# Which operand stands still: the sequence DFT of a Fourier block, with the DFT matrix stationary in place of the data

## The chip, the cores and the metric

The kernel runs on one core of a Trainium2 chip. The metric is the device time of one execution in microseconds. Five engines matter here: TensorE (PE) does the matmuls, VectorE (DVE) and ScalarE (ACT) do elementwise work and move results out of the accumulators (PSUM), GpSimd (POOL) does elementwise work in SBUF alone, and SyncE (SP) issues every DMA. Each engine works through its own instructions in the order in which they were written; between engines there are semaphores.

## The reference

One layer: a Fourier mixing block and a gated feed-forward block, each behind a layer norm, on 2048 tokens of 448 columns.

```python
# x: (1, 2048, 448); layernorm(x) = (x - mean) / sqrt(var + 1e-5), over the 448 columns
xn = layernorm(x)
a = einsum("bsd,ed->bse", xn, dft_hid_re)
b = einsum("bsd,ed->bse", xn, dft_hid_im)
h = x + einsum("ts,bse->bte", dft_seq_re, a) - einsum("ts,bse->bte", dft_seq_im, b)
hn = layernorm(h)
out = h + (gelu(hn @ w_gate) * (hn @ w_up)) @ w_down        # w_gate, w_up: 448 x 1792
```

All arrays are 32-bit floats. The matrices are inputs; the kernel uses nothing of the DFT's structure.

## The kernel before

**Arithmetic.** Each 32-bit operand is split into a 16-bit high part and a 16-bit low part, the rest. ScalarE makes the high part (`hi_part`, L105), VectorE the low part (`lo_part`, L109 and L111). A product is three matmuls: high x high, high x low, low x high.

**Order of the two DFTs.** The kernel transforms along the sequence first: z = W x, with the real and the imaginary W (2048 x 2048 each), and then along the hidden axis, y = z_re C - z_im S. h = x + y.

**Sequence DFT (L346 to L442).** There are 16 chunks of 128 tokens to sum over, and before the change 4 blocks of 512 output tokens: 64 steps, step n = 16 b + c. In a step the stationary operand is a 128-column piece of `xs[c]` (x normalized, high or low), the moving one is W's 512 columns (`seq_w`). 448 columns are three pieces of 128 and one of 64. The three full pieces, real and imaginary, have an accumulator each: 18 matmuls a step (`seq_mm`, L416). The 64-column pieces of the real and the imaginary part share one accumulator, each in half of its partitions: six matmuls of 64 columns a step, done for four steps at a time (`seq_mm_rest`, L430). The result is transposed, hidden index on the partitions, which is what the hidden DFT needs as its stationary operand: `z_out` scales the accumulators and splits them into `z[b]`, 7 accumulators every 16 steps.

**Feeding it.** In each step SP loads W five steps ahead (`seq_load`, 512 KB, five buffers `wr`), ScalarE and VectorE split W three steps ahead (`seq_hi`, `seq_lo`, tiles `ws`), and in the first steps they also normalize x (`x_stats`, `x_norm`, `x_lo`). Steps 0 and 1 have their W in halves (`first_load`, `first_hi`, `first_lo`). 56 small transposes (L99) precede the first matmul.

**What else stands in the 64 steps.** Two tables say what is put where: `early[n]` before the matmuls of step n, `after[n, half]` behind each half of them. They hold
- the preparation of 14 weight tiles of the feed-forward block (`Weights`): tile k is loaded at step 13 + 3k, its sums (VectorE) are made at 17 + 3k, the splits at 18 + 3k and 19 + 3k, and the result is stored to DRAM at 19 + 3k;
- the hidden DFT of the blocks that are done: `hid_mm` (L481, 21 matmuls of 448 columns for 128 tokens), whose result is added to x in `hx` (L489), and `h_store`;
- for the first half of the tokens the layer norm, sums and splits of h (`ffn_stats`, `ffn_norm`, `ffn_sums`, `ffn_split`) and their turn by DMA transposes into `hops` (`ffn_transpose`, L285, four for each pair of 128-token groups).

A pair of 128-token groups is numbered p or (b, j), p = 2b + j, p from 0 to 7.

**After it.** The last block's four hidden products stand behind the loop (L1001), and then 56 `GateUp` tiles follow, t = 0 to 55 (gate and up projection by Strassen-like products X, Y and Z of 256 moving columns, L716). `GateUp.open` makes the first products of X and Y and two intermediate sums, `u1` (from X, ScalarE) and `u2` (VectorE); X's next product waits until u1 has read X. From t = 14 the down projection (L664) runs beside them.

**Memory.** SBUF is given out by pools. Pool `dft` (the right end of SBUF, 229,344 bytes down) belongs to the DFT; when it is closed, `fpool` takes the same end. A pool lays out its tags in the order of first use. `fpool` has `reuse_waits="tile"`: a tile in it waits for the tiles of the old pool that lie where it lies, each until its last reader is done.

Of the kernel before, what the change touches and what calls it, by code (L numbers as in the profile page):

```python
# [13 lines left out]
P = 128  # L14
# [6 lines left out]
TB = 512  # L21
NB = S // TB
# [10 lines left out]
def kernel(  # L33
# [9 lines left out]

# [54 lines left out]
    for k in range(56):  # L98
        PE.transpose(pw[:, k % 8, :], ident, ident)  # L99
# [246 lines left out]
    def x_stats(i):  # L346
        mv = stats(xt[i], f"x{i}")
        norm_x[i] = mv, root(mv, f"x{i}")

    def x_norm(i):  # L350
        mv, sd = norm_x.pop(i)
        xn = xt[i][:, 0, :]
        normed(xn, xn, mv, rstd(mv, sd, f"x{i}"), 0)
        xs[i] = dft.tile([P, 2, D], F16, name=f"xs{i}")
        hi_part(xs[i][:, 0], xn)

    def x_lo(i):
        lo_part(xs[i][:, 1], xt[i][:, 0, :], xs[i][:, 0])
# [3 lines left out]

    wr, ws = {}, {}

    def seq_load(n):
        wr[n] = dft.tile([P, 8 * P], F32, tag="wr", bufs=5, name=f"wr{n}")
        b, q, jj = n // NT, n // 2 % 8, n % 2
        nc.sync.dma_start(wr[n], w_seq[(2 * b + jj) * 8 + q])

    def seq_hi(n):  # L370
        if n % 2 == 0:
            ws[n // 2] = dft.tile([P, 2, 2, 8 * P], F16, tag="ws", bufs=4, name=f"ws{n // 2}")
        hi_part(ws[n // 2][:, 0, n % 2], wr[n], D_SC)

    def seq_lo(n):
        t = ws[n // 2][:, :, n % 2]
        lo_part(t[:, 1], wr[n], t[:, 0], D_SC)


    def first_load(c, jj):  # L380
        if c == 0:
            wr[jj] = dft.tile([P, 8 * P], F32, tag="wr", bufs=5, name=f"wr{jj}")
        if c == jj == 0:
            ws[0] = dft.tile([P, 2, 2, 8 * P], F16, tag="ws", bufs=4, name="ws0")
        cols = slice(c * P, (c + 1) * P)
        nc.sync.dma_start(wr[jj].rearrange("p (b t) -> p b t", b=4)[:, :, cols], w_seq[jj * 8][:, :, cols])

    def first_views(c, jj):
        cols = slice(c * P, (c + 1) * P)
        ts = [wr[jj], ws[0][:, 0, jj], ws[0][:, 1, jj]]  # L390
        return [t.rearrange("p (b t) -> p b t", b=4)[:, :, cols] for t in ts]
# [9 lines left out]
    def seq_w(n, l, part):  # L401

        t = ws[n // 2][:, l].rearrange("p a (r g c t) -> p r c a g t", r=2, g=2, c=2)
        return t[:, part, n % 2]

    TERMS = ((0, 0), (1, 0), (0, 1))
    acc = {}

    def seq_mm(n, parts, terms=range(3)):

        b, c = divmod(n, NT)
        for part in parts:
            for k in range(3):
                for m in terms:
                    lx, lw = TERMS[m]
                    PE.matmul(  # L416
                        acc[b, 3 * part + k],
                        xs[c][:, lx, k * P : (k + 1) * P],
# [760 lines left out]
```

## Time and profile before

| | |
|---|---|
| median of 3 runs | 723.78 us (723.65 to 723.87) |
| profiled execution, its own time | 724.0 us |
| its span, first to last instruction | 722.2 us |
| PE busy | 716.9 us (99%) |
| PE weight loads (beside the matmuls) | 497.6 us (69%) |
| VectorE busy | 520.5 us (72%) |
| ScalarE busy | 276.8 us (38%) |
| GpSimd busy | 237.4 us (33%) |
| DMA queue of the program | 138.99 MB, 58.0% of 16 engines |
| granted TensorE clock, mean | 1.000 |

How to read the profile's lines. A group's line names the source line, engine and operation, what is written and read (out<-in), partitions x elements and type, and the count; then busy time in us, mean ns of one, the idle time of that engine just before, and what ended it ("<-"). A line of the timeline has start and length in us, and "x2" where equal neighbours were merged. In the chain that ended last each piece is followed back to what released it. "SPq" is SP's queue of DMA issues; "to landing" is the time from a DMA's issue to its end. L105, L109 and L111 are helpers and appear for many tiles, so the tile's name tells them apart.

### The profile page before, as it was taken

How to read it: one execution, taken by the hardware profiler on the slowest of the kernel's cores; microseconds unless marked ns; L12 is line 12 of the kernel's file. 1: busy time of each engine (PE TensorE's matmuls, PEld its weight loads, DVE VectorE, ACT ScalarE, POOL GpSimd, SP SyncE). 2: the span in 40 equal slices, each digit the busy share in tenths (PEclk: the TensorE clock that was granted, in tenths of full speed). 3: DMA queues.
4: the chain of work that ended last, by engine and by line, in shares of the span. 5: the costliest groups of instructions: out<-in, count | busy, mean ns of one | idle time of the engine just before them, and what ended most of it. 6: DMA issues, size and time to landing. Idle time of an engine off the chain costs nothing.

```text
span 722.2 us, 13457 instructions
## 1 busy us (share of the span) xinstructions
PE 716.9 (99%) x5309; PEld 497.6 (69%) x5309; DVE 520.5 (72%) x1074; ACT 276.8 (38%) x542; POOL 237.4 (33%) x277
## 2 busy tenths in 40 slices
PE   9999999999999999999999999999999999999998
PEld 5444444444444444444488889999999999999998
DVE  6888657486674956440567768788787877988787
ACT  4444704157132452130344443443444324444331
POOL 0000000000000001000137855577676776858541
PEclk9999999999999999999999999999999999999999
DMA  8766565678657876712643454756538486565401
GB/s 278 229 226 218 185 216 194 201 218 275 233 197 213 292 234 248 291 58 71 253 151 132 158 207 174 199 180 201 187 120 250 164 215 229 172 238 205 154 26 52
DMA packets 63663, 139.84 MB, mean 194 GB/s; under 512 B 30320, under 2 KB 39664, under 8 KB 63600
## 3 DMA queue, kind: packets, MB, share of 16 engines
q1 hardware_dynamic: 63600, 138.99, 58.0%
q8 instruction: 41, 0.67, 0.4%
q14 instruction: 22, 0.18, 0.1%
HBM read 112.23 MB, written 20.19 MB: 183 GB/s over the span
## 4 chain that ended last, share of the span: by engine, by line
PE 96%; DMA 2%; DVE 1%; ACT 0%; issue 0%; SPq 0%; DVEq 0%
PE acc L416 33%; PE pY L716 14%; PE acc_d L664 11%; PE pZ L716 9%; PE pX L716 9%; PE y L481 9%; PE acc L430 6%; PE last_a L921 2%; PE last_X L879 1%; PE last_tr L879 1%; DMA x<-in_x_dram 1%; DMA wr<-in_w_seq_dram 0%; DVE ws L111 0%; PE last_Y L921 0%; DVE xs L109 0%
## 5 line engine op out<-in xcount | busy, mean ns | idle before, releaser
L416 PE MATMUL acc<-ws,xs 128*128 128x512 f16 x1152 | 254.2, 379 | 0.6 <-DVE xs L109 0.3
L416 PEld LDWEIGHTS <-xs 128*128 128x128 f16 x1152 | 111.2, 98 | 139.4 <-issue 6.1
L716 PEld LDWEIGHTS <-gw 128*128 128x128 f16 x1911 | 186.6, 98 | 19.6 <-issue 0.7
L203 POOL TENSOR_TENSOR wd_s<-wd 128x448 f32<-128x448 f32 x7 | 7.9, 1134 | 351.9 <-DVE gu_w L111 274.1
L716 PE MATMUL pY<-hops,gw 128*128 128x256 f16 x833 | 114.0, 273 | 0.3 <-DVE u L726 0.2
L664 PE MATMUL acc_d<-wd,dn_w 128*128 128x224 f16 x882 | 105.1, 259 | 0.0
L111 DVE SCALAR_TENSOR_TENSOR ws<-wr,ws 128x1024 f16<-128x1024 f32 (+1 forms) x66 | 77.9, 1187 | 15.3 <-ACT ws L105 15.3
L105 ACT ACTIVATE ws<-wr 128x1024 f16<-128x1024 f32 (+1 forms) x66 | 66.2, 1020 | 58.1 <-DMA wr<-in_w_seq_dram 28.7
L664 PEld LDWEIGHTS <-dn_w 128*128 128x128 f16 x882 | 85.1, 98 | 2.8
L716 PE MATMUL pX<-hops,gw 128*128 128x256 f16 x539 | 74.9, 273 | 0.0
L716 PE MATMUL pZ<-hops,gw 128*128 128x256 f16 x539 | 73.7, 273 | 0.0
L726 DVE SCALAR_TENSOR_TENSOR u<-pY,u 128x256 f32<-128x256 f32 x112 | 46.9, 419 | 28.6 <-ACT c L790 18.6
L481 PE MATMUL y<-wh,z 128*128 128x448 f16 x336 | 65.7, 352 | 0.0
L489 DVE SCALAR_TENSOR_TENSOR hx<-y,hx 128x448 f32<-128x448 f32 x16 | 10.0, 624 | 76.2 <-PE y L481 76.2
L754 ACT ACTIVATE u<-pX 128x256 f32<-128x256 f32 x56 | 21.4, 383 | 89.1 <-PE pX L716 89.0
L481 PEld LDWEIGHTS <-z 128*128 128x128 f16 x336 | 32.8, 98 | 31.6 <-issue 0.4
L109 DVE TENSOR_TENSOR dn_w<-dn_s,dn_w 128x640 f16<-128x640 f32 x42 | 53.0, 1261 | 1.4 <-ACT dn_w L105 1.0
L783 POOL TENSOR_TENSOR hh<-hh,g 128x256 f32<-128x256 f32 x42 | 31.0, 739 | 64.3 <-DVE hh L726 50.7
L767 ACT ACTIVATE g<-pX 128x256 f32<-128x256 f32 x56 | 21.5, 384 | 75.0 <-PE pX L716 69.7
L792 POOL TENSOR_TENSOR hh<-hh,c 128x256 f32<-128x256 f32 x42 | 40.5, 964 | 17.1 <-ACT c L790 17.1
L430 PE MATMUL acc<-ws,xs 128*64 128x512 f16 x384 | 44.7, 381 | 0.0
L810 POOL TENSOR_TENSOR dn_s<-hh 128x256 f32<-128x256 f32 x42 | 43.4, 1034 | 0.0
(115 smaller groups left out, 862.8 us busy)
## 6 DMA issues: line engine op xcount, KB each, us to landing
gw<-w_dram SPq DMA_DIRECT2D x49, 896.0 KB, 4.8
wr<-in_w_seq_dram SPq DMA_DIRECT2D x62, 512.0 KB, 5.9
w_dram<-gu_w SPq DMA_DIRECT2D x14, 896.0 KB, 4.7
gu_raw<-in_w_gu_dram SPq DMA_DIRECT2D x28, 384.0 KB, 5.6
wd<-in_w_down_dram SPq DMA_DIRECT2D x14, 448.0 KB, 5.1
x<-in_x_dram SPq DMA_DIRECT2D x16, 224.0 KB, 2.7
hx<-in_x_dram SPq DMA_DIRECT2D x8, 448.0 KB, 6.9
h_dram<-hx SPq DMA_DIRECT2D x8, 448.0 KB, 3.1
```

The source lines that it names most:

```text
L105: A.activation(dst, src, AF.Copy, scale=scale)
L109: V.tensor_sub(dst, src, hi)
L111: V.scalar_tensor_tensor(dst, src, scale, hi, op0=ALU.mult, op1=ALU.subtract)
L416: PE.matmul(acc[b, 3 * part + k], xs[c][:, lx, k * P : (k + 1) * P], seq_w(n, lw, part), start=c == 0 and m == 0, stop=c == NT - 1 and m == 2,
L430: PE.matmul(acc[b, 6][64 * part : 64 * part + 64, :], xs[c][:, lx, 3 * P :], seq_w(n, lw, part), start=c == 0 and m == 0, stop=c == NT - 1 ...
L481: PE.matmul(y[:, :D], z[b][:, lz, k, i * P : (i + 1) * P], wh[:, lw, k, :], start=k == 0 and m == 0, stop=k == 6 and m == 2,)
L664: PE.matmul(acc[k // 2][:, k % 2 * HD : (k % 2 + 1) * HD], a_of(la, a), b_of(lb, b), start=first and m == 0 and k % 2 == 0, stop=last and ...
L716: PE.matmul(ps, w[:, wl, wa + ws, :], ops[:, m + ms, :], start=first and n == 0, stop=last and n == len(terms) - 1, skip_group_check=True,)
L726: V.scalar_tensor_tensor(dst, ps, SC, other, op0=ALU.mult, op1=ALU.add)
L783: G.tensor_mul(c21, c21, self.g1)
L792: G.tensor_mul(c22, c22, self.c12)
L810: G.tensor_sub(s[:, 2:4], t[:, 1:4:2], t[:, 0:4:2])
```

## The change

The operands of the sequence DFT change places. A tile of W (128 x 128) is now stationary, and all 448 columns of x move, high or low: 24 matmuls a step, 448 columns each, none of half width. The result has tokens on its partitions.

- Pairs 0 and 1 are summed together in steps 0 to 15 (eight accumulators, the eighth in the bank of the hidden DFT), two chunks of x for every two tiles of W. After that each pair has eight steps: four for the real part, four for the imaginary part, two accumulators each. W's tiles are loaded in two DMAs of 2 KB rows.
- `z_out` writes rows into `zs` (every four steps, two accumulators), and `z_turn` turns a pair's rows into `z` by four DMA transposes on SP's queue. The pair's hidden products follow two steps later.
- x's high part comes from x by one activation with scale and bias, x itself is normalized by another (for chunk 0 by VectorE), the terms come in another order, and 48 small transposes are left of 56.
- wh is ordered like the new z (real part, then imaginary part), in three pieces.
- Of the hidden products behind the loop those of pair 6 move into it, and pair 7's go between GateUp tiles 2 and 3. `down_prep` starts one tile later. `u2`, `g1`, `u3`, `c12` and the drain's copies move from pool `late` to `fpool`, and `late` opens at t = 3.

```diff
-    for k in range(56):
+    for k in range(48):
         PE.transpose(pw[:, k % 8, :], ident, ident)
...
+    def x_hi(i):
+        r = norm_x[i][2]
+        xs[i] = dft.tile([P, 2, D], F16, name=f"xs{i}")
+        A.activation(xs[i][:, 0], xt[i][:, 0, :], AF.Identity, scale=r[:, 3:4], bias=r[:, 4:5])
...
+    N_STEPS = NT + 8 * (NP - 2)
     def seq_load(n):
         wr[n] = dft.tile([P, 8 * P], F32, tag="wr", bufs=5, name=f"wr{n}")
-        b, q, jj = n // NT, n // 2 % 8, n % 2
-        nc.sync.dma_start(wr[n], w_seq[(2 * b + jj) * 8 + q])
+        if n < NT:
+            nc.sync.dma_start(wr[n].rearrange("p (b t) -> p b t", b=4), w_seq[8 * (n % 2) + n // 2])
+            return
+        p, part, qq = step_of(n)
+        for i in range(2):
+            dst = wr[n][:, i * 4 * P : (i + 1) * 4 * P].rearrange("p (g t) -> p g t", g=2)
+            nc.sync.dma_start(dst, w_seq[8 * p + 2 * qq + i][:, 2 * part : 2 * part + 2, :])
+    def ws_tile(n):
+        ws[n] = dft.tile([P, 2, 8 * P], F16, tag="ws", bufs=6, name=f"ws{n}")
...
-    def seq_mm(n, parts, terms=range(3)):
...
-    def seq_mm_rest(ns):
...
+    def seq_mm(key, w, block, c, terms=range(3)):
+        for m in terms:
+            lw, lx = TERMS[m]
+            PE.matmul(
+                acc[key][:, :D],
+                w[:, lw, block * P : (block + 1) * P],
+                xs[c][:, lx, :],
+                start=c == 0 and m == 0,
+                stop=c == NT - 1 and m == 2,
+            )
+    def z_out(p, part, g):
+        if p not in zs:
+            zs[p] = dft.tile([P, 2, 2, 2 * D], F16, tag="zs", bufs=2, name=f"zs{p}")
         sc = 1.0 / (X_SC * D_SC)
+        ps = acc.pop((p, part, g))[:, :D]
+        hi, lo = [zs[p][:, g, l, part * D : (part + 1) * D] for l in range(2)]
+        hi_part(hi, ps, sc)
+        lo_part(lo, ps, hi, sc)
+    def z_turn(p):
+        z[p] = hidp.tile([P, 2, 7, 2 * P], F16, tag="z", name=f"z{p}")
+        for g in range(2):
+            for l in range(2):
+                nc.sync.dma_start_transpose(z[p][:, l, :, g * P : (g + 1) * P], zs[p][:, g, l, :])
...
-    for b in range(NB):
-        for j in range(2):
-            n = (b + 1) * NT + 1 + 6 * j
...
-            for g in range(2):
-                at(after, (n + 2 * g, 0), lambda b=b, i=2 * j + g: hid_mm(b, i, ps_tr, "tr"))
...
+    for p in range(NP - 1):
+        b, j = divmod(p, 2)
+        n = (16, 21)[p] if p < 2 else 8 * p + 8
+        at(early, n - 1, lambda b=b, j=j: h_tile(b, j))
+        at(after, (n, 0), lambda p=p: z_turn(p))
+        for g in range(2):
+            at(after, (n + 2 + g, 0), lambda p=p, g=g: hid_mm(p, g))
+        at(early, n + 4, lambda b=b, j=j: ffn_stats(b, j, hp[b, j]))
+        at(early, n + 4, lambda b=b, j=j: h_store(b, j))
+        if b < 2:
+            at(early, n + 4, lambda b=b, j=j: ffn_norm(b, j, hp[b, j]))
+            at(early, n + 5, lambda b=b, j=j: ffn_sums(b, j))
+            at(early, n + 6, lambda b=b, j=j: ffn_split(b, j))
+            for k in range(4):
+                at(after, (n + 7 + k // 2, k % 2), lambda b=b, j=j, k=k: ffn_transpose(b, j, (k,)))
...
+        for half in range(2):
+            for key, unit, block, c, terms in one[half * len(one) // 2 : (half + 1) * len(one) // 2]:
+                seq_mm(key, ws[unit], block, c, terms)
+                if c == NT - 1 and 2 in terms and (n < NT or block in (5, 7)):
+                    z_out(*key)
+            for what in after.get((n, half), ()):
                 what()
+    z_turn(NP - 1)
...
     def ftile(tag, bufs, name, n=TQ):
-        return (fpool if tag == "u1" else late).tile([P, n], F32, tag=tag, bufs=bufs, name=name)
+        return fpool.tile([P, n], F32, tag=tag, bufs=bufs, name=name)
...
-    for i in range(4):
-        if i < 2:
-            down_prep(i)
-        hid_mm(NB - 1, i, *((ps_tr, "tr"), (ps_seq, "mm"))[i % 2])
...
+    down_prep(0)
...
+            if t in (2, 3):
+                hid_mm(NP - 1, t - 2)
+                ffn_moments(NB - 1, 1, hp[NB - 1, 1], t - 2)
+            if t == 3:
+                h_store(NB - 1, 1)
+                ffn_rstd(NB - 1, 1)
+                hid.close()
+                late = ctx.enter_context(tc.tile_pool(name="late", bufs=1, reuse_waits="tile"))
```

More of the change, by code (lines that the diff above doesn't have):

```diff
@@ L399, in first_lo @@
         lo_part(lo, src, hi, D_SC)
[L401 to L406, printed above, removed]
+    TERMS = ((0, 0), (0, 1), (1, 0))
     acc = {}
[L409 to L422 removed]
```

213 lines of the change are left out of this document (105 added, 108 removed).

## The prediction

> **What bounds the kernel now.** I read the page first: busy time, clock row, chain that ended last.
>
> ```profile
> span 722.2 us, 13457 instructions
> PE 716.9 (99%) x5309; PEld 497.6 (69%) x5309; DVE 520.5 (72%) x1074; ACT 276.8 (38%) x542; POOL 237.4 (33%) x277
> PEclk9999999999999999999999999999999999999999
> PE 96%; DMA 2%; DVE 1%; ACT 0%; issue 0%; SPq 0%; DVEq 0%
> ```
>
> TensorE is busy 716.9 of 722.2 us at the full granted clock, and 96% of the chain is PE. So the time falls by what PE no longer executes, and rises by every stretch in which PE is made to wait. The profiled execution took 724.0 us (its span and 1.8 us around it), against a median of 723.78 for the runs shown. The sum is made on 724.0. Within 0.2% (1.45 us) I count as no change, which is about what a measurement of this kernel can tell.
>
> Next the groups of instructions. The "mean ns of one" is a latency of overlapping matmuls, so I divide the busy time by the count, and check that in the chain, where a run of equal matmuls stands with its length.
>
> ```profile
> L416 PE MATMUL acc<-ws,xs 128*128 128x512 f16 x1152 | 254.2, 379 | 0.6 <-DVE xs L109 0.3 <-ACT xs L105 0.2
> L481 PE MATMUL y<-wh,z 128*128 128x448 f16 x336 | 65.7, 352 | 0.0
> L430 PE MATMUL acc<-ws,xs 128*64 128x512 f16 x384 | 44.7, 381 | 0.0
> ```
> ```profile
> 44.70 15.65 PE acc L416 x72
> 60.35 2.71 PE acc L430 x24
> 135.98 3.97 PE y L481 x21
> ```
>
> The chain gives 15.65/72 = 217.4 ns for a 512-column matmul, 2.71/12 = 226 ns for a pair of half-column ones (a pair takes little more than one full product), and 3.97/21 = 189.0 ns for a 448-column one. The last form has a 128x128 stationary operand changed for every matmul and 448 contiguous moving columns, among the same transfers: it is just the form that the new sequence DFT takes.
>
> **The change part by part: the DFT's matmuls.** Before, four steps are 72 matmuls and 12 pairs: 15.65 + 2.71 = 18.36 us, 4.59 a step, 293.8 us for 64. After, a step is 8 blocks x 3 terms = 24 matmuls of 448 columns, 24 x 0.189 = 4.54 us, 290.3 for 64. In columns it is a draw (1152 x 512 + 192 x 512 = 1536 x 448). All that is won is the price of a column: 217.4/512 = 0.425 ns (in the pairs 0.441) against 189.0/448 = 0.422. That is **-3.5 us**. Bounds: 0, if the dearer column belongs to the stage's traffic and stays, and -7, if moving x is as much cheaper again; I take the 448-column row itself.
>
> A sentence by itself: the Trainium skill, "TensorE: Matmul & The Clock Gate" (section "Wait — 56ns, not 53.3ns?"), gives N/2.4 + 2.5 ns for a warm matmul of N columns, thus 215.8 and 189.2 ns. By it the stage would go from 1344 x 215.8 = 290.0 to 1536 x 189.2 = 290.6 us, no gain at all; the 448-column row agrees with it, the 512-column row does not.
>
> **The start.**
>
> ```profile
> 6.68 8.09 PE L416 MATMUL acc<-ws,xs 128*128 128x512 f16 x36 [0.21 <-ACT xs L105]
> 16.12 4.50 PE L416 MATMUL acc<-ws,xs 128*128 128x512 f16 x19
> 20.89 3.84 PE L416 MATMUL acc<-ws,xs 128*128 128x512 f16 x17 [0.27 <-DVE xs L109]
> 26.08 15.91 PE L416 MATMUL acc<-ws,xs 128*128 128x512 f16 x72
> ```
> ```profile
> 4.69 0.63 ACT L105 ACTIVATE ws<-wr 128x512 f16<-128x512 f32 x1
> 5.19 0.16 DVE L137 SCALAR_TENSOR_TENSOR r_x<-r_x 128x1 f32<-128x1 f32 x1
> 6.06 0.56 ACT L105 ACTIVATE xs<-x 128x448 f16<-128x448 f32 x1
> L224 ACT ACTIVATE xn_h<-hx,nb_h,r_h 128x448 f32<-128x448 f32 x8 | 5.7, 754 | 2.3 <-DVE nb_h L222 2.2
> ```
>
> Steps 0 to 3 last from 6.68 to 26.08, 19.40 us against 18.36 at the steady rate: 1.04 us of waits for x. The new order wants one W half and x's high part for the first matmul, and takes that part from x itself by an Identity activation (with scale and bias, 754 ns in its only row) instead of a normalization on VectorE and a 0.56 us copy. r_x ends at 5.35, W's first half at 5.32, so it runs 5.4 to 6.15: PE starts 0.5 us sooner. VectorE sheds the normalization of every later x as well, and ScalarE, 38% busy by the page, has room for it. I expect one wait of 0.3 us to stay (step 1, W's second columns). **-1.2 us** (0 to -1.8). The eight warming transposes less only end before x is ready.
>
> **The turn of z.** Before, z leaves PSUM in the layout that the hidden DFT needs, and its products stand 1 to 9 steps later. Now a pair's two token blocks leave as rows (zs), four DMA transposes of 128x896 turn them, and the first hidden product is due 2.5 steps, 11.3 us, after the pair's last matmul. z's evictions keep their volume (28 x 512 against 32 x 448 columns), at the rows
>
> ```profile
> L105 ACT ACTIVATE z<-acc 128x512 f16<-128x512 f32 x28 | 16.7, 597 | 34.6 <-PE acc L416 25.1 <-PE acc L430 8.5
> L111 DVE SCALAR_TENSOR_TENSOR z<-acc,z 128x512 f16<-128x512 f32 x28 | 18.2, 690 | 28.2 <-ACT z L105 28.2
> ```
>
> but they now come every four steps, not every sixteen, and each holds VectorE in its order until PE ends that step. What lies between two of them must fit four steps, 18.15 us. I take pair 3, whose turn stands after step 31 beside the FFN work of pair 2. VectorE has in steps 28 to 31 what these rows span (from one W low part to the third after it: three W low parts, one Weights tile's sums and two splits, one pair's statistics, norm, sums and low parts; 118.04 - 103.64 = 14.40 us), and another W low part (1.21) and pair of Weights splits (1.28):
>
> ```profile
> 103.64 1.21 DVE L111 SCALAR_TENSOR_TENSOR ws<-wr,ws 128x1024 f16<-128x1024 f32 x1
> 114.75 1.28 DVE L111 SCALAR_TENSOR_TENSOR gu_w<-gu_s,gu_w 128x512 f16<-128x512 f32 x2
> 118.04 1.21 DVE L111 SCALAR_TENSOR_TENSOR ws<-wr,ws 128x1024 f16<-128x1024 f32 x1
> ```
>
> 16.9 us, from about 1.2 us after step 27 (the eviction above), with some 0.5 us of waits for ScalarE's high parts (an estimate): done 0.5 us after step 31's end. Only then can SP go on: its queue has, ahead of z's transposes, the store of that Weights tile, the next tile's two loads, hx, two of pair 2's transposes, W's two loads and a third transpose. Their pitch, from the queue's own rows:
>
> ```profile
> 98.24 0.76 SPq L474 DMA_DIRECT2D hx<-in_x_dram  x1
> 104.12 1.10 SPq L368 DMA_DIRECT2D wr<-in_w_seq_dram  x2
> 116.06 0.33 SPq L337 DMA_DIRECT2D w_dram<-gu_w  x1
> 116.43 1.38 SPq L304 DMA_DIRECT2D gu_raw<-in_w_gu_dram  x2
> 117.86 0.78 SPq L368 DMA_DIRECT2D wr<-in_w_seq_dram  x1
> 141.01 2.62 SPq L285 DMA_TRANSPOSE hops<-xs  x2
> ```
>
> 0.4 + 1.4 + 0.5 + 2 x 1.35 + 1.1 + 1.35 = 7.4; then z's high half 1.35; its low half is issued at 0.5 + 7.4 + 1.35 = 9.3 us after step 31. From issue to landing:
>
> ```profile
> L285 SPq DMA_TRANSPOSE hops<-xs x32: 1216/1442/4272, 118.7 to 590.6; - x32
> DMA to landing us min/median/max: 2.4/6.0/8.4
> ```
>
> With the median 6.0 it lands at 15.3, due 11.3: **+4.0 us** of an idle PE (0.4 at 2.4, 6.4 at 8.4; transposes whose issue stretches to 4.27 make it more). Pair 4, after step 39, has no transposes of pair 3 ahead but one, yet the store in SP's way belongs to step 40: VectorE ends it about 1.3 (evictions) + 1.2 (W) + 0.4 (wait for ScalarE) + 1.3 (splits) = 4.2 us after step 39; 4.2 + 0.4 + 1.4 + 1.35 + 1.35 = 8.7, + 6.0 = 14.7: **+3.4 us** (0 to 5.8). Pairs 0, 1, 5 and 6 have no FFN split or store beside their turn; pair 2 has one transpose ahead and lands 1 to 2 us in time. W's loads sit behind the blocked queue too, but are issued five steps ahead: no cost, as long as a burst takes under 20 us. None of these can be a gain: before, PE doesn't wait there. That W now comes in 2 KB rows by twice as many issues costs SP 0.5 us a step and PE nothing.
>
> **The end of the DFT.** Before, the four last hidden products (16 us) lie between DFT and GateUp:
>
> ```profile
> 348.11 2.10 SPq L607 DMA_DIRECT2D gw_first<-w_dram  x4
> 349.31 16.06 PE L481 MATMUL y<-wh,z 128*128 128x448 f16 x84
> L754 ACT ACTIVATE u<-pX 128x256 f32<-128x256 f32 x56 | 21.4, 383 | 89.1 <-PE pX L716 89.0
> 369.19 1.20 PE pY L716 x11
> ```
>
> Now GateUp(0) follows at once, two products move to t = 2 and 3 unchanged, and g1, u2, u3 and c12 move to fpool. The pools hand out addresses in the order of first use. By the tiles' sizes dft ends with zs (two of 7,168 bytes) and s (5,120) below 229,344: the odd zs lies at 217,056 to 224,224. fpool's u1 begins 10,752 bytes below its end, at 218,592. So u1 and u2 of GateUp(0) are laid over zs of pair 7, whose four transposes have just begun, and must wait for all four. (That a tile here waits for the tiles beneath it and no more shows in gw_first, issued at 348.11, ahead of the DFT's end.) Call that end E. The evictions of zs take 0.05 + 0.54 + 0.6: the last low half is there at E + 1.25; SP issues at E - 1.6, - 0.3, + 1.05, + 2.4. DMA is quiet there, so I take a landing from the nearest quiet row (768 columns):
>
> ```profile
> L285 SPq DMA_TRANSPOSE hops<-xs x1: 1302/1302/1302, 141.0 to 141.0; - x1
> DMA to landing us min/median/max: 3.3/3.3/3.3
> ```
>
> 3.3, and 0.3 for one block more: E + 6.0, and u1 in 0.38: E + 6.4. PE can do 18 matmuls of 256 columns first (1.20/11 = 0.109 each, 1.96 us), then X's second product waits for u1 to have read X. **+4.4 us** (3.2 to 6.8 with the 2.4 and 6.0 landings). ScalarE's wd halves, now ahead of u1 without the hidden products' cover, lie within that wait; without it they would cost under 1 us. gw_first's loads come behind the transposes and are due 11 us later, plus the wait: hidden. The later wd steps, each one tile further back, are due only at t = 14, wh's new load order only at step 18: nothing.
>
> **The sum.** 724.0 - 3.5 - 1.2 + 4.0 + 3.4 + 4.4 = **731.1 us**, said as 731.0, +1.0%.
>
> **The rivals.** (1) *The turns are in time*: pairs 3 and 4 cost nothing because SP reaches their transposes 4 us sooner (VectorE ahead of PE at steps 31 and 39, or landings of 2 us). It decides at 11.3 us from the pair's last matmul to the landing. Then 724.0 - 4.7 + 4.4 = 723.7: no change. For it: the quiet landing of 3.3; against it: 16.9 of 18.15 us booked on VectorE in those steps. (2) *Nor is u1 held*: zs and u1 don't meet, or the transposes end within 2 us of E: 724.0 - 4.7 = 719.3, faster. With the turns late but u1 free: 726.6. (3) *The clock falls in the gaps*: three waits of 3 to 4.5 us on an engine that had none over 0.3. The start shows a slow phase:
>
> ```profile
> 1.37:2.37 1.00, 1.00 (x10) 1.00 0.55 154
> 5.37:6.37 1.00, 1.00 (x20) 1.00 0.96 250
> ```
>
> 10 to 12 transposes a us at first, 20 at the end, over 4 us: some 1.6 us lost for each time PE starts cold, up to 4.8 in all: 735.8. This trace has no gap after which one could see it. The same page of the Trainium skill (section "HAM oscillation — how this bites in real kernels") has the clock halve after an idle window of some 3.4 us; no run here shows it yet. (4) *The 512-column matmuls are no slower by shape*: no gain of 3.5 us, 734.5.
>
> **How the numbers follow.** Forecast, both turns late and the end too, 727 to 736: 0.50. Clock or columns on top of it, (3) and (4), 734 to 739: 0.14. Turns in time (1), 723.7: 0.13. Late turns but a free u1, 726.6: 0.07. Neither (2), about 719.3: 0.16. Slower are the first two and the fourth, 0.71; the same is (1), 0.13; faster is (2), 0.16. The range from 719 to 738 leaves out about half of (2) and half of (3) and (4), 0.15; the forecast's own is 727 to 736.
>
> **What would show it.** Right: y's product of pairs 3 and 4 waiting 3 to 5 us for a DMA into z, PE idle 4 us shortly after the DFT with u1 waiting for a transpose, 24 DFT matmuls in 4.54 us, PE's first DFT matmul at 6.1 to 6.3. Wrong: z's transposes landing within 11 us at each pair, no gap at GateUp(0), a clock row under 9, PE waiting for ws (then SP or DMA, not z, is the bound), or a first DFT matmul later than 6.7.

## The result: 2.3% slower, not 1%

The changed kernel takes 741.05 us (median of 5 runs, 739.49 to 741.21) against 723.78 us: 1.023 times as long, with an interval of 1.0215 to 1.0245. The prediction was 731.0 us with a range to 738. The direction was right; the size was 10 us short. The page of the changed kernel, by its span, busy time, clock row and chain:

```profile
span 739.3 us, 13609 instructions
PE 718.7 (97%) x5301; PEld 517.6 (70%) x5301; DVE 517.1 (70%) x1064; ACT 293.4 (40%) x564; POOL 236.5 (32%) x277
...
PEclk9999999999799999999999999999999999999999
...
PE 88%; SPq 4%; DMA 3%; DVE 3%; ACT 1%; issue 1%; DVEq 0%; ACTq 0%
```

TensorE is busy 718.7 us, 1.8 us more than before although its products got cheaper, and its share of the chain fell from 96 to 88%; SP's queue (SPq), DMA and VectorE take 10% of it. One slice of the clock row reads 7, where before every one read 9. So two things are to be found: waits, and matmuls that ran slowly. TensorE's timeline has both; a row is start, length, instructions and count, and in brackets the idle time before it with what ended it:

```profile
6.46 53.80 PE L443 MATMUL acc<-xs,ws 128*128 128x448 f16 x281
...
103.42 18.32 PE L443 MATMUL acc<-xs,ws 128*128 128x448 f16 x96
121.58 4.13 PE L508 MATMUL y<-wh,z 128*128 128x448 f16 x21
...
155.63 31.94 PE L443 MATMUL acc<-xs,ws 128*128 128x448 f16 x168
195.39 0.93 PE L508 MATMUL y<-wh,z 128*128 128x448 f16 x2 [7.81 <-DMA z<-zs]
196.61 6.11 PE L508 MATMUL y<-wh,z 128*128 128x448 f16 x19 [0.29 <-DMA z<-zs]
202.56 4.70 PE L443 MATMUL acc<-xs,ws 128*128 128x448 f16 x24
...
211.07 31.94 PE L443 MATMUL acc<-xs,ws 128*128 128x448 f16 x168
244.42 0.55 PE L508 MATMUL y<-wh,z 128*128 128x448 f16 x2 [1.40 <-DMA z<-zs]
...
248.82 4.70 PE L443 MATMUL acc<-xs,ws 128*128 128x448 f16 x24
...
372.36 1.23 PE L771 MATMUL pX<-hops,gu_w 128*128 128x256 f16 x5 [3.94 <-ACT u L809]
...
378.12 0.71 PE L771 MATMUL pX<-hops,gu_w 128*128 128x256 f16 x5
...
394.09 0.71 PE L771 MATMUL pY<-hops,gw_first 128*128 128x256 f16 x5 [0.81 <-DVE u L781]
...
403.92 0.71 PE L771 MATMUL pY<-hops,gw_first 128*128 128x256 f16 x5 [1.44 <-DVE u L781]
```

Read row by row, against what each should have been:

- **Rate.** From 103.42 to 121.58 96 products take 18.16 us, 189.2 ns each; 1,536 of them 290.6 us against 293.8 before: -3.2 us.
- **Start.** The first product of the DFT starts at 6.46, against 6.68: -0.2 us. From there to 90.94 the first 444 products take 84.48 us, 0.5 more than at 189.2 ns each, where before the first four steps lost 1.04: another -0.5. Together -0.7 us.
- **Pair 3.** y was due at 155.63 + 168 x 0.1892 = 187.41. It waits 7.81 us for z, runs two products, waits 0.29, and then needs 5.95 us (196.61 to 202.56) for 19 products that take 3.60 at full clock. It ends at 202.56 instead of 191.38: +11.2 us, 2.9 of them (0.55 + 2.35) slow matmuls.
- **Pair 4.** Due at 211.07 + 31.79 = 242.86, the next DFT product starts at 248.82 instead of 246.83: +2.0 us.
- **End of the DFT.** GateUp(0) starts at 366.30; after 18 products (1.97 us) X's second product was due at 368.27 and starts at 372.36. The 39 products from there to 378.12 take 5.76 us instead of 4.25. Together +5.6 us, 4.1 of wait and 1.5 of slow matmuls.
- **Units 2 and 3 of gate and up.** 0.81 and 1.44 us of waits for u: +2.3 us.

-3.2 - 0.7 + 11.2 + 2.0 + 5.6 + 2.3 = +17.2 us, against 17.1 between the spans (739.3 and 722.2).

The slow matmuls go with the granted clock. A row gives the stretch, its length, TensorE's busy time (instructions), the granted clock, then DMA's busy share and GB/s:

```profile
191.20:201.40 10.20, 5.72 (x15) 0.50 0.92 200
372.10:375.40 3.30, 3.04 (x15) 0.50 0.96 369
```

From 187.2 to 191.1, from 201.5 to 211, and on either side of the second stretch the same view gives 1.00.

**Why pair 3 was so late** is read from the chain in time order (start, length, piece) between 160 and 197 us, and from the waits of SP and ScalarE from 158 to 225 (us in total, times, longest):

```profile
164.68 2.00 SPq L284
...
172.41 2.69 DMA hops<-xs
...
181.01 0.33 SPq L336
...
191.64 1.26 SPq L466
...
193.00 3.56 DMA z<-zs
```

```profile
SPq L336 <- DVE gu_w L110: 16.8, 2, 11.6
```

```profile
ACT xs L104 <- DMA hops<-xs: 8.6, 1, 8.6
```

The store of a Weights tile (line 336) and of a pair (519) stand in SP's queue until VectorE has made their data (11.6 us ahead of the Weights store at 162.08, 5.2 ahead of the next one at 181.01), and pair 1's FFN transposes (284) stand behind the first of them, issued from 164.68 on. The last lands at 175.1. Until then ScalarE holds pair 2's split, because its tile xs is the one buffer that pair 1's transposes read: 8.6 us. VectorE waits 3.6 and 0.7 us for ScalarE, the next store waits for VectorE and leaves SP only at 181.01, 4.9 us after step 31 has ended (176.06); and z's transposes come behind that, at 191.64. Theory C calls this the ring: store, transposes, split, store. It is what the trace suggests; the runs below test it against theory A, that the FFN transposes of pairs 1 and 2, now three steps apart instead of six, crowd the queue by their number, and theory B, that the turn is slow of itself.

### The profile page after: what moved, and what is told of

It reads as the page before. It is cut to its first block, busy times and chain, and to the rows that moved or that the text cites. A ratio compares the mean times of both kernels' runs of the same rounds, so it can differ in the third digit from the quotient of the medians.

```text
span 739.3 us, 13609 instructions
## 1 busy us (share of the span) xinstructions
PE 718.7 (97%) x5301; PEld 517.6 (70%) x5301; DVE 517.1 (70%) x1064; ACT 293.4 (40%) x564; POOL 236.5 (32%) x277
## 4 chain that ended last, share of the span: by engine, by line
PE 88%; SPq 4%; DMA 3%; DVE 3%; ACT 1%; issue 1%; DVEq 0%; ACTq 0%
PE acc L443 32%; PE pY L771 14%; PE acc_d L719 11%; PE y L508 9%; PE pX L771 9%; PE pZ L771 9%; SPq L284 2%; PE last_a L976 2%; DMA x<-in_x_dram 1%; DMA z<-zs 1%; PE last_X L934 1%; PE last_tr L934 1%; SPq L303 1%; DVE ws L110 1%; DVE gu_w L110 0%
## 5 line engine op out<-in xcount | busy, mean ns | idle before, releaser
L443 PE MATMUL acc<-xs,ws 128*128 128x448 f16 x1536 | 293.4, 353 | 0.1
L443 PEld LDWEIGHTS <-ws 128*128 128x128 f16 x1536 | 150.4, 98 | 140.5 <-issue 0.6
L508 PE MATMUL y<-wh,z 128*128 128x448 f16 x336 | 69.3, 362 | 9.8 <-DMA z<-zs 9.8
L104 ACT ACTIVATE zs<-acc 128x448 f16<-128x448 f32 x32 | 17.2, 541 | 102.2 <-PE acc L443 92.8
L110 DVE SCALAR_TENSOR_TENSOR zs<-acc,zs 128x448 f16<-128x448 f32 x32 | 19.4, 623 | 48.1 <-ACT zs L104 48.0
```

Of the source, the lines that this page charges most:

```text
L104: A.activation(dst, src, AF.Copy, scale=scale)
L110: V.scalar_tensor_tensor(dst, src, scale, hi, op0=ALU.mult, op1=ALU.subtract)
L443: PE.matmul(acc[key][:, :D], w[:, lw, block * P : (block + 1) * P], xs[c][:, lx, :], start=c == 0 and m == 0, stop=c == NT - 1 and m == 2,)
L508: PE.matmul(y[:, :D], z[p][:, lz, k, g * P : (g + 1) * P], wh[:, lw, k, :], start=k == 0 and m == 0, stop=k == 6 and m == 2,)
```

## The experiments

Each kernel was timed against the kernel before on the same chip (723.78 us beside the changed kernel, 723.94 to 724.21 beside the others). "Left" is TensorE's longest waits in the profiled execution, those of the first 25 us left out.

| kernel | median us | ratio to before (interval) | left |
|---|---|---|---|
| changed kernel | 741.05 | 1.023 (1.0215 to 1.0245) | 7.81, 3.94, 1.44, 1.40 |
| hidden products later | 735.76 | 1.0163 (1.0148 to 1.0178) | 5.62, 3.93, 1.44 |
| zs elsewhere | 735.64 | 1.0165 (1.0150 to 1.0180) | 7.71, 1.45, 1.22 |
| pair 2's FFN chain later | 734.85 | 1.0143 (1.0117 to 1.0169) | 4.15, 2.11, 1.90 |
| pair 7's statistics later | 741.02 | 1.0234 (1.0217 to 1.0251) | 7.78, 3.92, 1.96 |
| stores on GpSimd | 733.55 | 1.0132 (1.0113 to 1.0150) | 3.87, 2.31, 1.45 |
| W's loads on GpSimd | 759.60 | 1.0488 (1.0473 to 1.0502) | 18.43, 6.70, 3.93 |
| combination | 723.93 | 0.9993 (0.9984 to 1.0002) | 2.04 |
| combination, statistics spread | 720.14 | 0.9947 (0.9935 to 0.9960) | under 0.3 |
| the same, FFN chain not moved | 721.16 | 0.9961 (0.9949 to 0.9973) | 3.66 |
| the same, stores on SP | 722.40 | 0.9975 (0.9963 to 0.9986) | 2.05 |
| before, W contiguous | 728.57 | 1.0062 (1.0046 to 1.0077) | 0.46 |
| before, full for half columns | 720.43 | 0.9952 (0.9938 to 0.9965) | under 0.3 |

**Hidden products later.** The turns stay; the products that need them move.

```diff
         at(after, (n, 0), lambda p=p: z_turn(p))
+        n += {3: 2, 4: 1}.get(p, 0)
         for g in range(2):
             at(after, (n + 2 + g, 0), lambda p=p, g=g: hid_mm(p, g))
```

> Pair 3's hidden products and all that follows them (moments, norm, split, its FFN transposes) stand two steps later (9.1 us of DFT), pair 4's one step later (4.5 us); the turns of z stay where they are. Theory: the 7.81 us and 1.40 us that TensorE waited for z are pure lateness, and the 2.5 us of slow matmuls after the first wait go with it, so both waits vanish, nothing else becomes late, and the time falls by 11.3 + 2.0 to about 728 us (726 to 730). Rival: the wait only moves, because what comes after the hidden products is what sets the next turn; then a wait of several us stands before another pair's products and the time stays above 735 us.

The time fell by 5.3 us to 735.76, less than half of what the theory wanted: the rival was right on the size, and both waits for z had gone all the same. What took their place, a wait of 5.62 us before the second y product, is read from VectorE's rows, ScalarE's and SP's queue:

```profile
203.92 1.23 DVE L110 SCALAR_TENSOR_TENSOR ws<-wr,ws 128x1024 f16<-128x1024 f32 x1 [7.12 <-ACT ws L104]
...
209.93 0.62 DVE L516 SCALAR_TENSOR_TENSOR hx<-y,hx 128x448 f32<-128x448 f32 x1
```

```profile
202.83 1.06 ACT L104 ACTIVATE ws<-wr 128x1024 f16<-128x1024 f32 x1 [7.45 <-DMA wr<-in_w_seq_dram]
```

```profile
198.18 1.99 SPq L399 DMA_DIRECT2D wr<-in_w_seq_dram  x4
```

The second y product reuses the first one's accumulator and waits for VectorE to add it into hx. VectorE reaches hx at 209.93 because it stood 7.12 us for ScalarE's W part, which stood 7.45 us for a load of W issued at 198.18, behind z's four transposes and one of pair 2's. In the changed kernel VectorE was just as late (it stood 7.54 us for ScalarE's W part until 194.52), hidden behind TensorE's own wait for z: time given to one consumer showed the next.

**zs elsewhere.** `zs` is allocated ahead of W's tiles, so its two buffers no longer lie under u1.

```diff
             wr[jj] = dft.tile([P, 8 * P], F32, tag="wr", bufs=5, name=f"wr{jj}")
+            if jj == 0:
+                zs_tile(0)
             ws_tile(jj)
```

> The two buffers of zs are allocated at the head of the DFT's pool, so they lie under W_down's last tiles instead of under u1; no instruction is added or taken away. Theory: u1 then waits for no transpose of zs7, the 3.94 us before X's second product fall below 1 us (ScalarE still does two down-weight parts ahead of u1), the slow matmuls behind the gap go too, and the time falls by about 5 us to 736 us (735 to 737). Rival: the next thing is just as late (another tile under u1, ScalarE's queue), the idle time stays over 2.5 us and the time over 738.5 us.

735.64 us, 5.4 less. The wait before X's second product is 0.43 us, and the five products behind it take the usual 0.55 us from start to start instead of 1.02:

```profile
367.74 0.71 PE L776 MATMUL pX<-hops,gu_w 128*128 128x256 f16 x5 [0.43 <-ACT u L814]
```

The edit adds and takes away no instruction, only addresses differ. In the changed kernel u1 itself had waited for the transposes of zs:

```profile
371.93 0.38 ACT L809 ACTIVATE u<-pX 128x256 f32<-128x256 f32 x1 [3.40 <-DMA z<-zs]
```

That u1 was held by the transposes of zs beneath it is shown by the two together.

**Pair 2's FFN chain later.**

```diff
         if b < 2:
+            n += 3 if p == 2 else 0
             at(early, n + 4, lambda b=b, j=j: ffn_norm(b, j, hp[b, j]))
```

> Pair 2's norm, sums, split and FFN transposes stand three steps later (behind the turn of z of pair 3, and six steps behind those of pair 1, as far apart as those of before); its hidden products and everything of z stay. Theory A: pair 3's z is late because the FFN transposes of pairs 1 and 2 and the waits for their one buffer stand ahead of it in the one DMA queue; then the 7.81 us fall below 1.5 us, the slow matmuls behind them go, and the time falls by 9 to 11 us to about 731 us (729.5 to 733). Theory B: the turn is late of itself (four issues of 1.3 us each and a landing of 4 us against two steps); then the 7.81 us stay within 2 us and the time stays above 738 us. Between: both shares are read from the idle time that is left.

734.85 us, 6.2 less; A had expected 731. Pair 3's wait fell from 7.81 to 2.11 us, not below 1.5; what moving the chain took away is 5.7 us of it:

```profile
189.63 0.55 PE L508 MATMUL y<-wh,z 128*128 128x448 f16 x2 [2.11 <-DMA z<-zs]
190.40 5.45 PE L508 MATMUL y<-wh,z 128*128 128x448 f16 x19 [0.21 <-DMA z<-zs]
195.68 4.70 PE L443 MATMUL acc<-xs,ws 128*128 128x448 f16 x24
```

```profile
182.17 8.37 SPq L466 DMA_TRANSPOSE z<-zs  x4
```

SP now issues z's four transposes from 182.17, not from 191.64. The four issues alone take 8.37 us, and the products behind a gap of only 2.11 us still run slowly: 19 in 5.28 us instead of 3.60. Behind pair 4's waits of 1.90 and 0.26 they don't (238.84 to 242.45, 3.61 us).

**Pair 7's statistics later.** Moments and root behind unit 8.

```diff
-                ffn_moments(NB - 1, 1, hp[NB - 1, 1], t - 2)
+            if t == 8:
+                ffn_stats(NB - 1, 1, hp[NB - 1, 1])
             if t == 3:
                 h_store(NB - 1, 1)
-                ffn_rstd(NB - 1, 1)
```

> The moments and the root of pair 7 stand behind unit 8 of gate and up instead of units 2 and 3. Theory: the 0.81 and 1.44 us that TensorE waited for u in units 2 and 3 come from the 0.8 us of moments ahead of it on VectorE and the two table loads of 1.28 us on ScalarE; they fall to under 0.5 us in all, the loads now lie beside other work, and the time falls by about 2 us to 739 us (738 to 740). Rival: the hidden product's own sum and W_down's split hold u; the idle time stays over 1.5 us in all, and the time within 1 us of 741.

741.02 us: nothing. The two waits went, and one of 1.96 us came at the new place. The theory's sum was wrong: in one lump the work had its price at this place too. Whether that is VectorE's order or ScalarE's table loads this run does not tell; the spread combination below does.

**Stores on GpSimd.** Both stores, and nothing else, are issued by another engine.

```diff
-            nc.sync.dma_start(w_dram[self.f], self.w)
+            G.dma_start(w_dram[self.f], self.w)
...
-        nc.sync.dma_start(h_dram[2 * q + j], hp[q, j])
+        G.dma_start(h_dram[2 * q + j], hp[q, j])
```

> The stores of the split gate and up weights (line 336) and of the hidden pairs (line 519) are issued by GpSimd instead of SP; nothing else changes. In the trace SP stood 7 us and more before such a store until VectorE had made gu_w, with W's loads and the transposes queued behind it, while ScalarE and VectorE waited for those loads. Theory C: this ring (store waits for VectorE, W's loads wait for the store, VectorE waits for W's loads) is what makes pair 3 late; then the 7.81 us fall below 3 us, and the time falls by 6 to 10 us to 731 to 735 us. Theory A (crowded FFN transposes and their one buffer alone): the store costs little, the 7.81 us stay above 6 us and the time above 738.5 us.

733.55 us, 7.5 less, with the FFN chains as close as ever. Pair 3's wait is gone altogether, and ScalarE no longer waits for xs's buffer at all; pair 4 waits 2.31 us, and its 21 products take 5.71 us (233.99 to 239.70) instead of 3.97:

```profile
PE y L508 <- DMA z<-zs: 2.3, 1, 2.3
```

```profile
153.22 3.91 SPq L284 DMA_TRANSPOSE hops<-xs  x2
158.32 3.05 SPq L284 DMA_TRANSPOSE hops<-xs  x2
...
181.86 5.94 SPq L466 DMA_TRANSPOSE z<-zs  x4
```

Pair 1's transposes are issued from 153.22 instead of 164.68, the last two at 158.32 instead of 171.15, and z's at 181.86 instead of 191.64. That is C's ring cut at the store. C and A aren't two causes, though: moving the chain cuts the same ring at the buffer (ScalarE doesn't wait for it in that run either), and each cut alone took 5.7 us or more from that wait. At pair 3 the number of the transposes did no harm once no waiting store stood in front of them. At pair 4 it is open: the issue of z's four took 10.38 us there (from 223.79), and what stretched it was not tried. Nor was either kind of store moved by itself. The Trainium skill, "DMA: Bandwidth & Descriptors" (section "SWDGE vs HWDGE vs iDMA"), gives plain transfers to SP or ScalarE and leaves GpSimd those that accumulate or cast; here the plain stores were better on GpSimd, by these 7.5 us, because a waiting store holds up only the queue that it is in.

**W's loads on GpSimd** instead of the stores.

```diff
-            nc.sync.dma_start(dst, w_seq[8 * p + 2 * qq + i][:, 2 * part : 2 * part + 2, :])
+            G.dma_start(dst, w_seq[8 * p + 2 * qq + i][:, 2 * part : 2 * part + 2, :])
```

> W's loads of steps 16 to 63 are issued by GpSimd instead of SP, so they stand behind neither the stores nor the transposes. Theory C: with the loads out of the ring ScalarE and VectorE no longer wait 8 to 11 us for wr around pair 3, the store comes in time, and the 7.81 us fall below 3 us: 731 to 735 us. Theory A: pair 3's turn is still queued behind the FFN transposes, which wait for the split and its buffer; the 7.81 us stay above 5 us, 737 to 741 us. A third way: GpSimd's own issue of 96 loads is slower than SP's, W comes late, TensorE waits in the DFT's own products, and the time rises above 742 us.

759.6 us, 18.6 more: a miss for all three (the third had the time above 742 us, but TensorE never waited in the DFT's own products). Taking the loads out of SP's queue did not cut the ring; the wait for the xs buffer grew:

```profile
ACT xs L104 <- DMA hops<-xs: 13.0, 1, 13.0
```

The split stood 13.0 us for its buffer (8.6 in the changed kernel), and the store behind it left SP at 184.70 instead of 181.01, 3.7 us later. Then three of pair 2's transposes took 13.54 us to issue (188.29 to 201.83), where in the changed kernel they and two loads took 7.25, and z's came at 201.93 instead of 191.64. The FFN transposes' landing went from a median of 4.7 to 7.8 us in that stretch, with W's loads now issued beside them; that these are the reason was not tried. GpSimd's own pace in issuing the loads did not show: TensorE never waited for W.

**The combination.** Hidden products of pairs 3 and 4 one step later, pair 2's chain three, zs elsewhere, stores on GpSimd, pair 7's statistics behind unit 9; where an edit differs from those above:

```diff
-        n += {3: 2, 4: 1}.get(p, 0)
+        n += {3: 1, 4: 1}.get(p, 0)
...
-            if t == 8:
+            if t == 9:
                 ffn_stats(NB - 1, 1, hp[NB - 1, 1])
```

> Together: the hidden products of pairs 3 and 4 and what follows them one step later, pair 2's FFN chain three steps later, zs at the head of the pool, the two kinds of stores on GpSimd, and the moments and root of pair 7 behind unit 9. Theory: the waits are separate and each of these takes its own away; from 741.05 go 11.3 (pair 3), 2.0 (pair 4), 5.0 (u1) and 1 to 2.3 (units 2 and 3), which gives 721 us (719 to 723.5), below the 723.8 of before by the 3.3 us that the shorter matmuls gain less the late start. Rival: VectorE's and ScalarE's streams, which ran at their limit around pair 3, put another wait in place of these (as they did with the hidden products two steps later); then a wait of over 3 us is left and the time stays above 725 us.

723.93 us, 17.1 less than the changed kernel but no better than before. The waits were separate, as the theory said, and one is left, of 2.04 us:

```profile
411.45 0.87 PE L778 MATMUL pY<-hops,gw 128*128 128x256 f16 x5 [2.04 <-DVE u L788]
```

```profile
410.98 0.41 DVE L788 SCALAR_TENSOR_TENSOR u<-pY,u 128x256 f32<-128x256 f32 x1
```

VectorE's rows: the moments from 406.08, the root's arithmetic to 408.67, then c, a W_down part of 1.32 us and a sum of 0.81 us, and only at 410.98 the u that TensorE wants. That sum falls in unit 10, so unit 9 was no good place; but behind unit 8, without the sum, the lump had cost 1.96 us too. ScalarE's two table loads of 1.28 us end at 406.30 and 409.27, well before.

**Combination, statistics spread.** One moment each ahead of the W_down parts in units 3 and 5, where VectorE had gaps of 0.95 us, the root alone behind unit 7, and the first W_down parts behind unit 0's u1.

```diff
+        if t in (3, 5):
+            ffn_moments(NB - 1, 1, hp[NB - 1, 1], (t - 3) // 2)
         if t + 1 <= 2 * NC:
             down_prep(t + 1)
...
+            if t == 7:
+                ffn_rstd(NB - 1, 1)
...
-    down_prep(0)
...
     cur.open()
+    down_prep(0)
```

> As the combination before (hidden products of pairs 3 and 4 one step later, pair 2's FFN chain three steps later, zs at the head of the pool, stores on GpSimd), but pair 7's two moments stand in the gaps of VectorE ahead of W_down's parts in units 3 and 5, its root alone behind unit 7, and the first down-weight parts behind unit 0's u1. Theory: the 2.04 us at unit 9 came from VectorE's order (1.6 us of moments, 0.7 of root, a W_down part and a sum all ahead of u), not from the table loads; spread out, no wait over 0.5 us is left, and the time falls from 723.9 to 721 us (720 to 722), a ratio to before of about 0.996. Rival: the two table loads of 1.28 us on ScalarE hold u wherever they stand; then a wait of 1.4 to 2 us stays at unit 7 or 8 and the time stays at 723 to 724 us.

720.14 us, 3.8 below before, interval 0.9935 to 0.9960. This version beats both kernels. TensorE's waits, all but one of 1.4 us before any data is there:

```profile
PE acc L450 <- DVE xs L108: 0.2, 1, 0.2
PE pY L778 <- DVE u L788: 0.2, 1, 0.2
```

The table loads are still there and cost nothing, so it was VectorE's order. With no wait left the time should be 723.9 less 3.2 and 0.7, 720.0: the account closes. (The 3.8 us against the combination are its wait of 2.04 us and 1.7 us lost behind it, where the granted clock read 0.50.)

**The same without moving the FFN chain, and with the stores on SP.** Each takes one part of the last one back.

```diff
-            n += 3 if p == 2 else 0
```

> The same without moving pair 2's FFN chain: its transposes stand again three steps behind those of pair 1. Theory C: once the stores no longer hold SP, the crowding of the FFN transposes costs little; TensorE waits for z less than 1 us in all and the time is within 1 us of the version with the chain moved. Theory A: the crowding is a cause of its own; a wait of over 2 us before the hidden products of pair 3 or 4 comes back and the time is 3 us and more longer.

```diff
-            G.dma_start(w_dram[self.f], self.w)
+            nc.sync.dma_start(w_dram[self.f], self.w)
...
-        G.dma_start(h_dram[2 * q + j], hp[q, j])
+        nc.sync.dma_start(h_dram[2 * q + j], hp[q, j])
```

> The fastest combination with both kinds of stores back on SP. Theory C (the stores' waits in SP's queue are the root of pair 3's lateness): with the FFN chain moved alone 2.11 and 1.90 us were left at pairs 3 and 4, which the one step (4.5 us) covers for z itself, but SP still waits for VectorE, W's loads behind it come late, and a wait of 2 us or more for hx or z comes back: 723 to 727 us. Theory A (crowded FFN transposes): with the chain moved and the step given no wait over 1 us is left, and the time is 720 to 721.5 us.

721.16 and 722.40 us. Without the move most runs stayed near 720 to 722.8, but the profiled one, the longest of seven at 725.48, had a wait of 3.66 us at pair 3; with the stores on SP one of 2.05 us stood at pair 4 in the profiled run (723.53 us):

```profile
203.76 5.63 PE L513 MATMUL y<-wh,z 128*128 128x448 f16 x21 [3.66 <-DVE hx L521]
```

```profile
246.36 5.82 PE L513 MATMUL y<-wh,z 128*128 128x448 f16 x21 [2.05 <-DVE hx L521]
```

Both are for hx, as with the hidden products later: just before, VectorE had stood 8.71 and 13.71 us for ScalarE's W part. So neither C nor A alone decides it: the stores are worth 2.3 us here (the intervals don't touch), the chain's place 1.0 on the median, which is not clear of noise (0.9949 to 0.9973 against 0.9935 to 0.9960), and 5 in the longest run.

**Where the 3.2 us of the products come from.** Two runs of the kernel before. In the first W's moving columns are read as one run of 512:

```diff
-        t = ws[n // 2][:, l].rearrange("p a (r g c t) -> p r c a g t", r=2, g=2, c=2)
-        return t[:, part, n % 2]
+        return ws[n // 2][:, l, n % 2, part * 512 : part * 512 + 512]
```

> The kernel before with W's moving columns read as one run of 512 instead of four runs of 128 (so it multiplies other columns of W; the count and shape of the matmuls stay). Theory: the 217.4 ns of its 512-column matmuls come from the four runs; they fall to about 216 ns, and with 1,152 of them the time falls by 1.5 to 2 us to 722 us. Rival: they belong to the shape of 512 columns; the mean stays within 0.3 ns of 217.4 and the time within 0.5 us of 723.8.

In the second one full product stands for each pair of half-column ones:

```diff
-                for part in range(2):
-                    PE.matmul(
-                        acc[b, 6][64 * part : 64 * part + 64, :],
-                        xs[c][:, lx, 3 * P :],
-                        seq_w(n, lw, part),
+                PE.matmul(
+                    acc[b, 6],
+                    xs[c][:, lx, D - P :],
+                    seq_w(n, lw, m % 2),
```

> The kernel before with one full product (128 columns of x stationary) in place of each pair of half-column products, so half of those columns' results are left out; 192 matmuls of 512 columns stand for 384 of half the rows. Theory: the 3.3 us that the new DFT gains are the price of the half-column products, not of 512 columns: in rows without them 63 matmuls take 13.61 us, 216.0 ns each, and each group of 24 halves takes 2.72 us for 12 pairs, with some 0.09 us more in the row ahead of it; then DFT's four steps fall from 18.36 to 84 x 0.216 = 18.14 us and the time by 3.3 to 3.5 us to 720.6 us (720.2 to 721.2). Rival: a 512-column matmul costs 217.4 ns wherever it stands; then the four steps stay at 18.26 us or above and the time within 1.6 us of before.

TensorE's rows of four steps, of before, then contiguous, then with full products:

```profile
196.97 13.77 PE L416 MATMUL acc<-ws,xs 128*128 128x512 f16 x63
210.58 4.14 PE L481 MATMUL y<-wh,z 128*128 128x448 f16 x21
214.55 2.11 PE L416 MATMUL acc<-ws,xs 128*128 128x512 f16 x9
216.58 2.78 PE L430 MATMUL acc<-ws,xs 128*64 128x512 f16 x24
219.30 6.00 PE L416 MATMUL acc<-ws,xs 128*128 128x512 f16 x27
```

```profile
198.63 13.77 PE L415 MATMUL acc<-ws,xs 128*128 128x512 f16 x63
212.24 4.14 PE L480 MATMUL y<-wh,z 128*128 128x448 f16 x21
```

```profile
194.94 13.76 PE L416 MATMUL acc<-ws,xs 128*128 128x512 f16 x63
208.54 4.14 PE L479 MATMUL y<-wh,z 128*128 128x448 f16 x21
...
212.51 2.11 PE L416 MATMUL acc<-ws,xs 128*128 128x512 f16 x9
214.46 2.75 PE L429 MATMUL acc<-ws,xs 128*128 128x512 f16 x12
217.05 5.99 PE L416 MATMUL acc<-ws,xs 128*128 128x512 f16 x27
```

From start to start 63 products take 13.61, 13.61 and 13.60 us: 216.0 ns each in all three, so the four runs of 128 columns cost nothing. (The first kernel is 4.5 us slower all the same. In the profiled run, the fastest of four at 726.34 us, its first product of the DFT starts 2.7 us later, after a wait of 1.85 us for a part of W; that covers that run's 2.3 us. The other three, 727.93 to 729.29 us, show a mean granted clock of 0.995 to 0.998 instead of 1.000; behind which gaps it fell is not known, since they have no trace.) The dear rows are those at the half columns: 9 products ahead of them take 2.03 us instead of 1.95, and 12 pairs 2.72 instead of 2.59 for 12 full products. With full products the four steps fall from 18.36 to 18.14 us and the time by 3.5 us to 720.43. That is the whole gain of the new DFT, which has no half columns: 1,344 x 216.0 ns = 290.3 us and 1,536 x 189.2 = 290.6 are the same.

## Why the prediction was right and wrong

The step that failed most is the size of pair 3's turn: 4.0 us in the sum, 11.2 measured. Behind it come units 2 and 3 of gate and up, put at nothing and measured at 2.3 us, and the clock, 4.4 us, left to a rival. Term by term:

**The products (-3.5; measured -3.2).** Right in size, wrong in cause, so the size was luck. The 217.4 ns came from a piece of the chain that ran up to the half columns, and so had their surcharge in it; in rows without them it is 216.0. The rule of the Trainium skill, "TensorE: Matmul & The Clock Gate" (section "Wait — 56ns, not 53.3ns?"), 215.8 and 189.2 ns, agrees with both rows after all; rival 4 had its premise right, yet the gain stayed, because it was never in the shape of 512 columns. For the pairs the same page (section "Measured speedup vs the span model") has about 4 ns for each further tile packed beside the first; here a pair takes 2.72/12 = 226.7 ns against 215.8 for the full product, 11 more.

**The start (-1.2; -0.7).** The chain of x was right. W's first half came later than in before: ScalarE's first part of it started at 4.99 instead of 4.69, so 6.46 instead of 6.1 to 6.3.

**Pair 3's turn (+4.0; +11.2).** The mechanism was right, z late behind stores and transposes in SP's queue, and the term was mis-sized in three steps. VectorE was booked by its busy time (16.9 of 18.15 us), done 0.5 us after step 31; it was done 4.9 after, because ScalarE had to wait 8.6 us for the one xs buffer and VectorE then 4.4 us for ScalarE, which no booking of busy time shows. SP's queue ahead of z was put at 7.4 us; from 181.01 to 191.64 it took 10.6, with two transposes at 4.88 us instead of 2.7. The landing was put at 6.0 us and was 3.56, which gave some of it back. And the slow matmuls, 2.9 us, were left to a rival. That W's loads behind the blocked queue cost nothing was true of TensorE alone: ScalarE and VectorE waited 7 us and more for them, which the run with the hidden products later brought to light.

**Pair 4's turn (+3.4; +2.0).** Right: the Weights store left SP at 235.68, 4.2 us after step 39, as booked. The landing was again shorter; z's transposes took 3.5 us on the median, not 6.0.

**The end (+4.4; +5.6).** Right in place, cause and wait (4.1 us); the slow matmuls are the rest. Moving zs, which adds and takes away no instruction, left 0.43 us of the wait and none of the slow matmuls.

**Units 2 and 3 (0; +2.3).** The failed step is "two products move to t = 2 and 3 unchanged". The products did; their sum, moments and root came with them onto VectorE, in a stage where u stands behind them in its order. Counting everything that moved with the products, engine by engine, would have found it.

**Rival 3, the clock.** It came true on top of the forecast: with a granted clock of 0.50, 2.9 and 1.5 us were lost behind two of the gaps, 4.4 in all, against the 4.8 allowed for three. The price of 1.6 us a gap was right for the second and half of the first; what failed is that it stood beside the sum and not in it, though three gaps of 3.4 to 4.4 us were forecast.

From 731.1 to 741.05: 7.2 at pair 3, 1.2 at the end, 2.3 in the units, 0.5 at the start, 0.3 in the rate, less 1.4 at pair 4, in all 10.1.

## What to carry to other kernels

Where one in-order queue carries both transfers that wait for an engine and transfers that the engine waits for, busy times don't tell when it is free: follow each wait around until it comes back to where it began, single buffers included, and put the transfers that wait onto a queue with nothing urgent behind them. A late operand must be given time at every consumer in the chain, or the next one shows the same lateness; here six moves, none of which takes away an instruction, turned 2.3% slower into 0.5% faster. And before a gain is put down to a shape, divide rows that hold only that shape.

## What the runs showed of the hardware

The clock fell behind shorter gaps than the prediction had in mind. Gaps of 2.04, 2.05, 2.11 and 2.31 us were each followed by about 1.7 us of lost time (21 products in 5.65 us instead of 3.97 behind the 2.05), and longer ones, from 3.66 to 18.43, by 1.5 to 2.9; gaps of 1.96, of 1.90 and 0.26, and of 1.40 us by none. The Trainium skill, "TensorE: Matmul & The Clock Gate" (section "HAM oscillation — how this bites in real kernels"), warns of gaps of more than about 3.4 us; in the profiled executions every gap from 2.04 us up was followed by a fall and none up to 1.96. Behind the gaps of 2.04 to 2.31 us the granted clock reads 0.50 for some 3.4 us (from 411.9 to 415.2 in the combination, 1.00 on either side), and half of that is the 1.7 us. A gap of 2 us need not bring a fall in each execution: of the combination's eleven runs seven show a mean granted clock of 0.997 and took 723.84 to 724.78 us, four show 1.000 and took 722.66 to 723.40, still 2.5 us and more above the median without the gap. Those four have no trace, so how long the gap was in them is not known. Behind the 2.11 us the first two products still took 0.55 us, as they did behind pair 4's 1.90, and the slow ones came after: the loss is not always read from the row right behind the gap.

SP's issue of a DMA transpose is not of one length: 1.25 us for one alone, 5.45 us for z's four in the changed kernel, 8.37 in the run with the FFN chain moved, 10.38 for pair 4's with the stores on GpSimd. What sets it these runs leave open.
